# Sparse attention and a soft mixture of experts on one core: local products grouped by key block, dense rows by PE transposes and products over 128 keys

## The chip, the core and the metric

The kernel runs on one NeuronCore of a Trainium2 chip. Its engines are TensorE (PE: matrix products, with weight loads listed apart as PEld), VectorE (DVE), ScalarE (ACT), GpSimd (POOL) and SyncE (SP, which here only starts DMAs). Each engine works through its own queue in order. SBUF is the working memory, PSUM takes the products of PE, and HBM is the main memory. The metric is the device time of one execution in microseconds, lower is better; everything is in float32.

## The reference

For 4 batches, 8 heads, 768 positions and 64 numbers a head, with key blocks of 32 positions (24 blocks):

```python
mask = abs(blk_i - blk_j) <= 1
mask |= (blk_i == 0) | (blk_j == 0) | (blk_i == 23) | (blk_j == 23)
for qb in range(24):
    for kb in sampled_blocks[qb]:        # 3 random key blocks per query block
        mask[qb block, kb block] = True
attn = softmax(where(mask, scale * q @ k.T, -1e9))
x = (attn @ v) as [3072, 512]            # all heads side by side

logits = x @ phi                         # 32 slots: 8 experts of 4
d = softmax(logits over the 3072 rows);  slot_input = d.T @ x
slot_out[e] = relu(slot_input[e] @ w1[e]) @ w2[e]      # w1 512x1024, w2 1024x512
out = softmax(logits over the 32 slots) @ slot_out
```

So query blocks 0 and 23 look at all 768 keys (dense rows), and each of the 22 others at 8 blocks of 32 keys: block 0, block 23, its own with its two neighbours, and three sampled ones. The sampled numbers are read at run time.

## The kernel before

**Local rows.** Two query blocks form a pair, and two pairs a tile of 128 rows of x (T); the first pair of a batch shares its tile with the dense rows. For each query block `stage_k` copies its 8 key blocks side by side into a buffer `kst`: the fixed ones on POOL (L455, L457), the sampled ones on ACT or POOL (L463, L465), for which `block_numbers` loads three numbers from SBUF into the engine's registers (L362). `stage_v` does the same for the sampled value blocks (`vrs`, L481, on POOL). `qk` (L536) makes the scores of a pair: 16 products of 64 rows of the array (a head's 64 numbers) by 32 columns (32 queries), 256 keys each, so that eight of them can lie on the array at once. DVE takes the row maximum (L551), ACT the exponential (L556), and DVE turns the probabilities in blocks of 32 x 32 (L563) into `ptt`. `av_heads` then multiplies them with the values (L628): per tile and half of the heads (r = 0, 1; a *set* below) 44 products with 64 rows, 130 streamed columns (two heads with a column of ones each), and 128, 64 or 32 output columns, depending on how many query blocks share the key block: the two global blocks serve all four query blocks of the tile, the two inner neighbours a pair, all others one query block. Values stand in `vfull` or `vtab` so that two heads fill 64 rows, with zeros for the other head.

**Dense rows.** Per batch there are two dense units, query block 0 and query block 23: scores by products of 64 x 32 with 384 keys (L732), maximum (L750), exponential (L763), DVE transposes into `ptd` (L767), and then, in one piece for both units, `dense`: 24 key blocks x 2 r x 2 g = 96 products of 64 x 64 with 130 columns (`avd`).

**After them** come per tile the division by the sums (L621 to L623, DVE), four transposes by PE (`mxt`, L823) whose result DVE or ACT copies out (`xT`, L374), and per four tiles the logits (`ml`), the exponentials of the dispatch softmax (`lt`, `md`) and the sums over rows (`ms`). The expert products (`pf`, `pso`) and the combination (`po`) follow at the end, fed by 33.5 MB of weights, of which part is loaded early into buffers that the attention has done with (`ktile`, `v0`, `ptd`).

**Order.** All of the attention is written as tasks (`add`). `Plan.run` puts them into one order with a list scheduler that walks through time with a cost per task, a key of due time (`OFF` shifts it by kind), buffer pools and a table of engine delays; the instructions are then recorded in this order, and each engine keeps its part of it. PSUM holds four score banks (`s`), one pair for the products with values (`av`), and two banks (`pt`) for everything that is turned or summed. A float32 product is recorded by the profiler as two products and two weight loads; a transpose is recorded as one of each.

Of the kernel before, what the change touches and what calls it, by code (L numbers as in the profile page):

```python
# [32 lines left out]
EARLYW, LATEW = ("ktile", "v0", "ptd"), ("ktile", "v1")  # L33
# [22 lines left out]
KW = {"ktile": 3, "v0": 6, "v1": 6, "ptd": 3}  # L56
# [6 lines left out]
SWITCH = 0.095  # L63
BACK = {"PE": 0.17, "DVE": -0.07, "ACT": -0.1, "POOL": -0.06, "SP": 0.0, "NONE": 0.0}
OFF = {"acc": 4.15, "av": 2.35, "av1": 4.1, "av2": -5, "avo": -4.9, "avo1": -5, "ce": 5, "cm": -2.05,
       "cn": 0.65, "dav": 3.7, "davo": -3.85, "dexp": 1.8, "do": 2.9, "dqk": 0.05, "dt": 4.55, "dtop": 0.85,
       "dtrn": -4.55, "exp": 2.7, "fix": 4.3, "ldq": 3.55, "lexp": -1.45, "lg": -0.55, "lo": -2.85, "lp": -5,
       "lt": 5, "ltop": -5, "qk": 0.85, "scl": 3.05, "smp": 3.9, "sum": -3.1, "top": -4.8, "trn": 0.2,
       "vst": 4.7, "xt": -2.8, "xto": -1}
# [5 lines left out]
class Task:  # L75
    def __init__(self, f, opts, deps, key, acq, byte, pre, pace, kind, mode, ni):
        self.pace, self.kind, self.mode, self.ni = pace, kind, mode, ni
        self.f, self.opts, self.deps, self.key = f, opts, [d for d in deps if d], key
        self.acq, self.byte, self.pre = list(acq), byte, pre
        self.start = self.fin = self.eng = None  # L80


class Plan:
# [6 lines left out]
    def add(self, f, opts, deps, key, acq=(), byte=0, pre=None, pace=False, kind=None, mode=None, ni=0):  # L90
        t = Task(f, opts if isinstance(opts, list) else [opts], deps, key + OFF.get(kind, 0.0), acq, byte, pre, pace,
                 kind, mode, ni)
        self.tasks.append(t)
        return t

    def run(self):
        tasks = self.tasks
# [3 lines left out]
        left = {t: len(t.deps) for t in tasks}  # L101
        ready = {t: 0.0 for t in tasks}
        out = {t: [] for t in tasks}
        for t in tasks:
            for d in t.deps:
                out[d].append(t)
# [3 lines left out]
        queue = {p: sorted([t for t in tasks if any(q == p for q, _ in t.acq)], key=lambda t: t.key)  # L110
                 for p in self.pools if p not in self.free}
        gives = {t: [] for t in tasks}
        spans, open_ = [], {}
        avail = [t for t in tasks if not t.deps]
        order = []
        while avail:
            cand = []
            for t in avail:
                r, ok, k = ready[t], True, {}
                for p, _ in t.acq:  # L120
                    i = (nxt[p] + k.get(p, 0)) % self.pools[p]
                    k[p] = k.get(p, 0) + 1
                    if (p in queue and queue[p][0] is not t) or held[p][i]:
                        ok = False
                        break
                    r = max(r, slot[p][i])
                if ok:
                    if t.pace:
                        r = max(r, paced)

                    st, e, d = min(((max(r, at[e]), e, d) for e, d in t.opts), key=lambda z: (z[0], z[0] + z[2]))
                    if e == "PE" and t.mode and t.mode[0] != mode:
                        d += SWITCH
                    cand.append((st, t.key, st + d, t, e, d))
            assert cand, [(t.key, t.opts) for t in avail][:8]
            soon = min(c[:3] for c in cand)
# [1335 lines left out]
```

## Time and profile before

| | |
|---|---|
| median of three runs | 306.38 us (304.79 to 307.34) |
| the profiled execution | 307.42 us, its span 305.6 us |
| PE busy in the span | 278.8 us, 7165 products and as many weight loads |
| DVE, ACT, POOL busy | 210.1, 165.1, 184.2 us |
| HBM read and written | 56.19 and 6.29 MB |

Times in the rows below are us from the span's start, unless marked ns. A product is pipelined, and its end is modelled, so PE's busy share says that PE has work, not that the array is full. "Idle before" of a group is the time in which its engine did nothing just before it, with what ended the wait.

### The profile page before, as it was taken

The page shows a single profiled execution, that of the slowest core. Times are in us where ns is not written, and L with a number is a line of the kernel's source. Part 1 is how long each engine was busy: PE and PEld are TensorE (multiplying, and loading weights), DVE is VectorE, ACT ScalarE, POOL GpSimd, SP SyncE. Part 2 cuts the span into 40 slices and gives each one's busy share as a digit, 9 for nine tenths or more (in the row PEclk, how much of TensorE's full clock was granted, in tenths as well). Part 3 has the DMA queues.
Part 4 walks back from the last instruction along what each step waited for, and adds up shares of the span by engine and source line. Part 5 has one row for each costly group of instructions (what it writes and reads, how often), then busy time and mean ns, then how long its engine had stood idle before and what let it go on. Part 6 is the DMA issues. An engine that isn't in the chain of part 4 may idle for free.

```text
span 305.6 us, 17578 instructions
## 1 busy us (share of the span) xinstructions
PE 278.8 (91%) x7165; PEld 193.4 (63%) x7165; DVE 210.1 (69%) x484; ACT 165.1 (54%) x507; POOL 184.2 (60%) x519
## 2 busy tenths in 40 slices
PE   7599998799999999989999899999999999999950
PEld 7158765476687666768676676877657763355540
DVE  4788968458999679878988669999779445012350
ACT  0876848463766875637758653876844142102440
POOL 2679489927954899885689894948957405000000
PEclk9869999999999999999999999999999999999996
DMA  7935677640156663035376510477788999999997
GB/s 244 400 116 161 177 209 222 167 126 3 38 158 193 185 184 105 5 88 139 105 197 190 144 50 28 131 209 208 211 221 288 397 400 408 407 409 407 389 343 263
DMA packets 31634, 63.61 MB, mean 208 GB/s; under 512 B 5313, under 2 KB 18754, under 8 KB 31554
## 3 DMA queue, kind: packets, MB, share of 16 engines
q1 hardware_dynamic: 31408, 62.37, 63.2%
q8 instruction: 56, 0.92, 1.3%
q14 instruction: 24, 0.20, 0.2%
q10 hardware_dynamic: 146, 0.13, 0.1%
HBM read 56.19 MB, written 6.29 MB: 204 GB/s over the span
## 4 chain that ended last, share of the span: by engine, by line
PE 64%; DMA 7%; issue 6%; POOL 6%; DVE 5%; POOLq 5%; ACT 4%; ACTq 1%; SPq 1%
PE av L628 24%; PE avd L628 7%; PE s L536 7%; PE pso L1278 5%; PE pf L1270 5%; PE sd L732 4%; POOLq L362 4%; DMA q<-in_qT_dram 4%; PE mxt L823 3%; PE ml L859 2%; PE ms L910 2%; POOL kst L465 2%; DMA ktile<-in_kT_dram 2%; POOL kst L457 2%; POOL vrs L481 1%
## 5 line engine op out<-in xcount | busy, mean ns | idle before, releaser
L481 POOL COPY vrs<-v 128x260 f32 x264 | 95.1, 407 | 21.2 <-PE av L628 12.2
L556 ACT ACTIVATE p<-s,nm 128x256 f32<-128x256 f32 x176 | 72.8, 483 | 11.3 <-DVE nm L551 9.8
L628 PE MATMUL av<-v,ptt 64*64 64x130 f32 (+2 forms) x1728 | 76.0, 288 | 0.1
L628 PEld LDWEIGHTS av<-v,ptt 64*64 64x64 f32 (+2 forms) x1728 | 50.5, 133 | 24.9 <-issue 16.8
L563 DVE STREAM_TRANSPOSE ptt<-p 128x512 f32<-128x512 f32 x88 | 57.5, 689 | 7.8 <-ACT p L556 7.2
L536 PE MATMUL s<-kst,q 64*32 64x256 f32 x1408 | 51.7, 380 | 7.4 <-POOL kst L465 4.3
L551 DVE TENSOR_REDUCE nm<-s 128x2 f32<-128x512 f32 x88 | 55.1, 680 | 4.6 <-PE s L536 4.2
L457 POOL COPY kst<-ktile 128x384 f32<-128x384 f32 x88 | 43.1, 509 | 11.9 <-PE s L536 11.0
L628 PE MATMUL av<-vrs,ptt 64*32 64x130 f32 x2112 | 46.6, 275 | 2.1 <-issue 1.9
L463 ACT ACTIVATE kst<-ktile 128x128 f32 x165 | 38.3, 310 | 9.1 <-PE s L536 8.7
L536 PEld LDWEIGHTS s<-kst,q 64*32 64x32 f32 x1408 | 29.9, 106 | 20.4 <-POOL kst L465 5.9
L628 PEld LDWEIGHTS av<-vrs,ptt 64*32 64x32 f32 x2112 | 35.6, 105 | 4.5 <-issue 4.3
L374 ACT COPY xT<-mxt 128x512 f32<-128x512 f32 (+1 forms) x25 | 14.1, 566 | 32.7 <-PE mxt L823 32.7
L465 POOL COPY kst<-ktile 128x128 f32 x99 | 24.9, 297 | 0.5 <-ACT kst L463 0.5
L498 ACT ACTIVATE q<-q 128x256 f32<-128x256 f32 x29 | 12.2, 427 | 21.4 <-DMA q<-in_qT_dram 21.4
L628 PE MATMUL avd<-v,ptd 64*64 64x130 f32 x768 | 22.8, 271 | 0.8 <-DVE x L623 0.6
L628 PEld LDWEIGHTS avd<-v,ptd 64*64 64x64 f32 x768 | 21.6, 132 | 2.4 <-PE s L536 2.0
L621 DVE TENSOR_SCALAR rs<-av 128x8 f32<-128x8 f32 (+2 forms) x28 | 4.5, 159 | 23.3 <-PE av L628 23.2
L732 PE MATMUL sd<-ktile,q 64*32 64x384 f32 x256 | 18.6, 524 | 1.1 <-ACT p L556 1.1
L500 POOL TENSOR_SCALAR q<-q 128x256 f32<-128x256 f32 x19 | 7.7, 409 | 18.9 <-DMA q<-in_qT_dram 14.1
L750 DVE TENSOR_REDUCE nm<-sd 128x1 f32<-128x384 f32 x32 | 16.3, 547 | 3.1 <-PE sd L732 3.1
L623 DVE TENSOR_TENSOR x<-av,rs 128x512 f32<-128x512 f32 (+2 forms) x28 | 16.9, 605 | 1.0
(124 smaller groups left out, 288.8 us busy)
## 6 DMA issues: line engine op xcount, KB each, us to landing
w<-in_w_dram SPq DMA_DIRECT2D x20, 512.0 KB, 9.9
v<-in_w_dram SPq DMA_DIRECT2D x12, 512.0 KB, 10.5
q<-in_qT_dram SPq DMA_DIRECT2D x47, 128.0 KB, 2.9
w<-in_w_dram SPq DMA_DIRECT2D x44, 128.0 KB, 3.3
out_dram<-ob SPq DMA_DIRECT2D x22, 256.0 KB, 4.4
ktile<-in_kT_dram SPq DMA_DIRECT2D x48, 96.0 KB, 3.1
v<-in_w_dram SPq DMA_DIRECT2D x24, 128.0 KB, 3.8
kw<-in_w_dram SPq DMA_DIRECT2D x6, 512.0 KB, 8.3
```

The costliest lines, as they stand in the source:

```text
L457: POOL.tensor_copy(out=st[:, :, w:w + 96], in_=kv[:, :, (i - 1) * BLK:(i + 2) * BLK])
L463: ACT.activation(out=st[:, :, o:o + BLK], in_=src, func=AF.Copy, scale=1.0)
L465: POOL.tensor_copy(out=st[:, :, o:o + BLK], in_=src)
L481: POOL.tensor_copy(out=st[:, :, j:j + 1, :], in_=vf[:, :, ds(t.vals[j], 1), :])
L536: PE.matmul(u.s[r][32 * p:32 * p + 32, j, :], lhsT=u.q[s_, p, j, :], rhs=kd[j][0][s_, p, :], start=True, stop=True)
L551: DVE.tensor_reduce(out=u.nm[r], in_=u.s[r], axis=AX.X, op=ALU.max, negate=True)
L556: ACT.activation(out=u.p[r][:, j, :], in_=u.s[r][:, j, :], func=AF.Exp, bias=u.nm[r][:, j:j + 1], scale=1.0)
L563: DVE.transpose(out=T.pt[r][:, :, 2 * w:2 * w + 2, :].rearrange("p k j q -> p j k q"), in_=u.p[r].rearrange("p j (k q) -> p j k q", k=8))
L623: DVE.tensor_tensor(out=x, in0=a[:, :, :, 0:D], in1=rs[lo:hi].unsqueeze(3).to_broadcast([hi - lo, 2, 2 * n, D]), op=ALU.mult)
L628: PE.matmul(av[:, r * 2 * D1:(r + 1) * 2 * D1].rearrange("p (a d) -> p a d", a=2), lhsT=lhsT, rhs=rhs, start=start, stop=stop)
L732: PE.matmul(u.s[r][k][32 * p:32 * p + 32, :], lhsT=T.dq.q[s_, p, j, :], rhs=kt[s_, p, 384 * k:384 * (k + 1)], start=True, stop=True)
L750: DVE.tensor_reduce(out=u.nm[r][:, k:k + 1], in_=u.s[r][k], axis=AX.X, op=ALU.max, negate=True)
```

## The change

- **Local products.** The sampled and fixed key blocks take a place in `kst` that depends on the query block's place t (0 to 3) in its tile: the window of three lies at 64 + 32 t, so a key block that several query blocks of a tile share has one place in all of them. `av_heads` sorts a set's products by width: those for four or three query blocks (128 or 96 columns), for two (64), for one (32); 42 in all. It writes them from wide to narrow, or (`up`) from narrow to wide, whichever begins with the shape that PE is in.
- **Dense rows.** A dense unit is now two heads per half with both dense query blocks (64 queries), not one query block of all heads. Scores are products of 64 x 64. The probabilities are turned by PE, six transposes of 128 x 128 per unit and r into two banks of `pt`, which DVE or ACT copies to SBUF. The products take 128 keys at a time from a new input `vden` (values with a column of ones, by key), 64 output columns and 65 streamed ones, in one task per unit (g = 0, 1).
- **Loads.** `vden` is loaded per batch in 16 pieces (3 whole ones in batch 0) into a buffer `vd`, in place of `ptd` and of nearly its size.
- **Block numbers** are loaded for both query blocks of a pair at once.
- **x** of two tiles is turned in one task of eight transposes.
- **Order.** The list scheduler is replaced by a written table of task numbers (`ORDER`, 1,375 of them), a + behind a number meaning the second choice of engine. A few costs are changed; they affect when registers are loaded and where waits for paced DMAs are put, not the order.

```diff
 class Plan:
...
+        for word in ORDER:
+            t = self.tasks[int(word.rstrip("+"))]
+            e, d = t.opts[word.count("+")]
...
+            if e == "PE":
+                t.up = t.turn and t.mode[0] != mode and t.mode[-1] == mode
...
     def stage_k(b, i, n, use, t_):
...
-            POOL.tensor_copy(out=st[:, :, w:w + 96], in_=kv[:, :, (i - 1) * BLK:(i + 2) * BLK])
+            POOL.tensor_copy(out=st[:, :, 64 + 32 * t_:160 + 32 * t_], in_=kv[:, :, (i - 1) * BLK:(i + 2) * BLK])
...
     def block_numbers(b, t, i, eng, most):
+        j = (i - 1) // 2
+        key = b, most, j, eng
+        if key not in both:
+            _, both[key] = nc.values_load_multi_w_load_instructions(
+                t[0:1, 2 * j + 1:2 * j + 3, :], engines=[{"ACT": E_.Activation, "POOL": E_.Pool}[eng]], min_val=0, max_val=most,
...
     def av_heads(T, rs_, up=False):
...
+        for r in rs_:
+            vb = lambda k: vt[:, :, VPOS(k), r, :]
+            for n, k in enumerate((0, NB - 1)):
+                put(wide, r, 0, n, nt, vb(k))
+            for n in range(nt + 2):
+                k, ts = i0 - 1 + n, range(max(0, n - 2), min(n, nt - 1) + 1)
+                if k in (0, NB - 1):
+                    continue
+                if len(ts) == 3 and ts[0]:
+                    put(low, r, ts[0], 2 + n, 1, vb(k))
+                    ts = ts[1:]
+                put((low, mid, wide)[len(ts) - 1], r, ts[0], 2 + n, len(ts), vb(k))
+        for n in ((1, 2, 0) if up else range(NR)):
             for r in rs_:
+                for t in range(nt):
+                    put(low, r, t, rest(t)[n], 1, us[t // 2].vst[t % 2].st[:, :, n, r, :])
+        todo = low + mid + wide if up else wide + mid + low
...
     def plan_dense(b, j, n):
...
-            def turn(t, r=r):
-                for k in range(2):
-                    DVE.transpose(out=ptd[r][:, 12 * k:12 * k + 12, j, :], in_=u.p[r][k])
...
+            def turn(t, r=r, z=z):
+                z.b = [bank("pdt") for _ in range(2)]
+                for c in range(NT):
+                    PE.transpose(z.b[c // 3][:, c % 3, :], u.p[r][c // 3][:, c % 3 * P:(c % 3 + 1) * P], ident)
+
+            def out(t, r, k, z):
+                if k == 0:
+                    u.pT[r] = pw.tile([P, 8, P], F32, tag="ptt", name="pdt", bufs=PTB)
+                evac(u.pT[r][:, 3 * k:3 * k + 3], z.b[k][:, 0:3], t.eng)
...
+                def dense(t, u=u, g=g, z=z):
+                    z.av = psA.tile([P, 2, 512], F32, tag="av", name="avd", bufs=1)
+                    for c in range(NT):
+                        for a in range(2):
+                            for r in range(2):
+                                PE.matmul(z.av[64 - 64 * r:128 - 64 * r, a, 0:D1], lhsT=u.pT[r][:, c, 64 * a:64 * a + 64],
+                                          rhs=vd[:, c, r * NP + 2 * g + a, :], start=c == 0, stop=c == NT - 1)
```

What stands on PE in the second batch from the first scores after its dense products on: the last `s` of a pair, the turn of a tile (`mxt`), and one set of local products (`av`). Names are output<-inputs, then output columns x streamed columns, then how often in a row. Before:

```order
L536 MATMUL s<-kst_96,q_98 32x256 x8
L823 MATMUL mxt<-ident,x 128x128 x4
L628 MATMUL av<-v_69,ptt 128x130 x4
L628 MATMUL av<-v_69,ptt 64x130 x8
L628 MATMUL av<-v_69,ptt 32x130 x8
L628 MATMUL av<-vrs_103,ptt 32x130 x2
```

And after, where one set of the tile ends and the next begins:

```order
L687 MATMUL av<-v_69,ptt 32x130 x6
L687 MATMUL av<-vrs_105,ptt 32x130 x2
...
L687 MATMUL av<-v_69,ptt 64x130 x6
L687 MATMUL av<-v_69,ptt 96x130 x2
L687 MATMUL av<-v_69,ptt 128x130 x8
L687 MATMUL av<-v_69,ptt 96x130 x2
L687 MATMUL av<-v_69,ptt 64x130 x6
L687 MATMUL av<-v_69,ptt 32x130 x6
```

A set now begins narrow and ends wide, and the next one runs back, so that the two 128-column runs meet without a change of shape; before, each set ran from wide to narrow.

The dense rows of the second batch on PE, before:

```order
L732 MATMUL sd<-ktile,q_98 32x384 x16
...
L536 MATMUL s<-kst_96,q_100 32x256 x8
L628 MATMUL avd<-v_69,ptd 64x130 x96
L536 MATMUL s<-kst_93,q_97 32x256 x8
```

And after:

```order
L804 MATMUL sd<-ktile,q_97 64x384 x8
L850 MATMUL pdt<-ident,pd 128x128 x6
...
L595 MATMUL s<-kst_94,q_99 32x256 x8
L850 MATMUL pdt<-ident,pd 128x128 x6
L873 MATMUL avd<-vd,pdt 64x65 x24
L850 MATMUL pdt<-ident,pd 128x128 x6
L595 MATMUL s<-kst_96,q_100 32x256 x8
```

The one block of 96 dense products has become two of 24, with four sets of six transposes ahead of and between them.

## Rows read from the trace of the kernel before

**Rows 1.** Stages: start:end, length, busy us (and count) by engine, PEclk, DMA share, GB/s.
```profile
18.00:75.00 57.00, 52.54 (x1572) 38.08 (x1568) 43.33 (x91) 36.45 (x111) 43.77 (x126) 0.98 0.52 148
75.00:132.00 57.00, 55.33 (x1715) 40.77 (x1699) 47.08 (x105) 37.34 (x122) 44.30 (x124) 1.00 0.42 116
132.00:189.00 57.00, 54.20 (x1654) 39.86 (x1660) 45.77 (x103) 36.04 (x110) 44.28 (x129) 1.00 0.46 126
189.00:246.00 57.00, 56.31 (x1629) 41.76 (x1614) 45.31 (x108) 31.22 (x99) 39.63 (x110) 1.00 0.77 232
246.00:291.00 45.00, 43.81 (x485) 22.70 (x485) 13.98 (x42) 12.54 (x33) 4.33 (x8) 1.00 1.03 405
```

**Rows 2.** PE in order of time, narrow stretches: start, us, engine, line, op, tiles, shape, count.
```profile
39.91 0.66 PE L823 MATMUL mxt<-ident,x 128*128 128x128 f32 x4
40.50 0.72 PE L628 MATMUL av<-v,ptt 64*128 64x130 f32 x8
82.61 5.62 PE L628 MATMUL avd<-v,ptd 64*64 64x130 f32 x192
88.15 2.06 PE L536 MATMUL s<-kst,q 64*32 64x256 f32 x64
249.85 1.08 PE L1133 MATMUL psS<-selw,sacc 128*128 128x32 f32 x8
```

**Rows 3.** Waits of PE: for whom, us in total, times, the longest.
```profile
PE s L536 <- POOL kst L465: 4.3, 3, 2.8
PE s L536 <- POOL vrs L481: 1.9, 1, 1.9
PE av L628 <- issue: 1.9, 6, 0.7
PE ml L859 <- issue: 1.0, 1, 1.0
PE ml L859 <- ACT xT L374: 0.7, 1, 0.7
```

**Rows 4.** The chain that ended last, 44 to 60 us: shares, and pieces of it.
```profile
by line: POOLq L362 28.6%; issue 18.3%; POOL vrs L481 17.9%; POOL kst L465 9.7%; PE s L536 8.8%; PE av L628 8.2%; POOLq L481 4.0%; POOL kst L457 3.1%; PE mxt L823 1.6%; POOLq L465 0.6%; POOLq L455 0.5%; POOL kst L455 0.5%
...
53.49 0.72 POOLq L362
```

**Rows 5.** From the page: busy us by engine, and the chain of the whole run by line.
```profile
PE 278.8 (91%) x7165; PEld 193.4 (63%) x7165; DVE 210.1 (69%) x484; ACT 165.1 (54%) x507; POOL 184.2 (60%) x519
...
PE av L628 24%; PE avd L628 7%; PE s L536 7%; PE pso L1278 5%; PE pf L1270 5%; PE sd L732 4%; POOLq L362 4%; DMA q<-in_qT_dram 4%; PE mxt L823 3%; PE ml L859 2%; PE ms L910 2%; POOL kst L465 2%; DMA ktile<-in_kT_dram 2%; POOL kst L457 2%; POOL vrs L481 1%
```

**Rows 6.** The same chain at other places: start, us, what.
```profile
15.87 2.35 PE sd L732 x16
...
20.06 1.86 DVE ptd L767 x4
...
135.84 1.04 issue
```

**Rows 7.** DMA queues: kind, packets, MB, share of 16 engines.
```profile
q8 instruction: 56, 0.92, 1.3%
```

**Rows 8.** Weight loads of PE by shape: count, busy us, mean ns, idle before.
```profile
L628 PEld LDWEIGHTS avd<-v,ptd 64*64 64x64 f32 x768 | 21.6, 132 | 2.4 <-PE s L536 2.0 <-DVE ptd L767 0.3
L628 PEld LDWEIGHTS av<-v,ptt 64*128 64x128 f32 x320 | 21.0, 184 | 9.7 <-issue 8.1 <-PE s L536 0.8 <-PE mxt L823 0.3
```

**Rows 9.** DVE and ACT groups by shape, and the page's group of transposes on PE.
```profile
L767 DVE STREAM_TRANSPOSE ptd<-pd 128x384 f32<-128x384 f32 x32 | 16.3, 552 | 1.3 <-ACT pd L763 1.2
L1376 DVE COPY ob<-po 128x512 f32<-128x512 f32 x10 | 6.7, 690 | 7.0 <-PE po L1374 7.0
L556 ACT ACTIVATE p<-s,nm 128x256 f32<-128x256 f32 x176 | 72.8, 483 | 11.3 <-DVE nm L551 9.8 <-issue 0.4 <-DVE ptt L563 0.3
L823 PE MATMUL mxt<-ident,x 128*128 128x128 f32 x96 | 15.9, 286 | 0.1
```

**Rows 10.** PE in the stretch of the lower clock: columns as in rows 1.
```profile
13.57:20.40 6.83, 5.71 (x79) 0.50 0.64 225
```

More of the change, by code (lines that the diff above doesn't have):

```diff
@@ L109, in run @@
         nxt = {p: 0 for p in self.pools}
[L110 to L136, printed above, removed]
-            eng = min(cand, key=lambda c: c[:3])[4]
-            st, _, en, t, e, d = min((c for c in cand if c[4] == eng and c[0] <= soon[0] + 0.05), key=lambda c: c[1:3])
-            avail.remove(t)
-            if e == "PE":
-                mode = t.mode[-1] if t.mode else None
-            t.start, t.eng, at[e] = st, e, en + BACK[e] + (0.11 if t.kind in ("qk", "dqk") else 0.0)
@@ L359, in load_v, with block_numbers @@
         return i
-    def block_numbers(t, i, eng, most):
-        _, vals = nc.values_load_multi_w_load_instructions(
-            t[0:1, i, :], engines=[{"ACT": E_.Activation, "POOL": E_.Pool}[eng]], min_val=0, max_val=most,
-            skip_runtime_bounds_check_because="block numbers lie in range by the definition of the input")
-        return vals
+    both = {}
+    def block_numbers(b, t, i, eng, most):
+        j = (i - 1) // 2
[3 more added lines that the diff above has]
+                t[0:1, 2 * j + 1:2 * j + 3, :], engines=[{"ACT": E_.Activation, "POOL": E_.Pool}[eng]], min_val=0, max_val=most,
+                skip_runtime_bounds_check_because="block numbers lie in range by the definition of the input")
+        o = (i - 2 * j - 1) * NR
+        return both[key][o:o + NR]
     def place(b, t):
@@ L671, in plan_av @@
+        seen = set()
+        for z in todo:
+            r, o, mm, g, lhsT, rhs = z
+            start = rows(z)[0] not in seen
+            assert all((q in seen) != start for q in rows(z))
+            seen.update(rows(z))
+            for q in rows(z):
+                left[q] -= 1
+            av_mm(T.av, o, mm, g, r, lhsT, rhs, start, not any(left[q] for q in rows(z)))
     def plan_av(T, n):
@@ new lines, in plan_dense @@
+            t_t = add(turn, ("PE", 0.6), [t_e], n + 0.3 + 0.01 * r, kind="dtp", mode="F", ni=12,
+                      acq=[("pt", b_use[0]), ("pt", b_use[1]), ("ptt", use)])
+            for k in range(2):
+                p_use[k].append(t_t)
+                t_o.append(add(lambda t, k=k, r=r, z=z, out=out: out(t, r, k, z), [("DVE", 0.5), ("ACT", 0.45)], [t_t] + t_o[-1:], n + 0.35 + 0.01 * r + 0.002 * k, kind="dto"))
+                b_use[k].append(t_o[-1])
+        T.dense.append((u, t_o, pt_use))
```

326 lines of the change are left out of this document (178 added, 148 removed), and 51 rows, old and new, of the table ORDER.

## The prediction

> **What bounds the kernel now.** I read the stages first [rows 1]. Batches 0 to 3 take the four stretches of 57 us between 18 and 246 us, with TensorE (PE) busy for 52.5 to 56.3 us of each, against 43 to 47 for VectorE (DVE) and 40 to 44 for GpSimd (POOL). From 246 us on the expert weights arrive at 405 GB/s while PE works through them; the change touches nothing there, so a gain or a loss must come out of the first 246 us and moves the rest as a block.
>
> PE's busy time is no measure of its work, so I looked at single products [rows 2]. A matrix product in float32 leaves two records. The 192 records of a dense product (`avd`, 64 rows by 64 columns of the array) start at 82.61 and the next task at 88.15: 5.54 us, and as four such tiles fit the array at once that is 48 steps of 0.115. The first eight 64 x 128 records of the local products take 0.72 in all, two at a time, so four steps; less the last one's own 0.27 the three starts between them lie 0.15 apart, the first of which also loads weights. Four transposes (`mxt`) take 0.66 with the last one's 0.29 in it, about 0.12 apart, and the next task begins 0.59 after their start: 0.44 for four steps of 0.11 and 0.15 for the change of shape. I carry 0.11 as the price of a step, whatever the width of the product, and 0.15 for each change of tile shape.
>
> Next, what PE waits for [rows 3]: POOL 4.3 + 1.9 us (2.8 of it one wait at the start), "issue" 1.9 + 1.0, ACT 0.7, and others alike. Idle counts only beyond the modelled end of a product, so each is worth some 0.2 us more. The chain of waits says more about POOL: in 44 to 60 us, 28.6% of the chain is POOLq L362 [rows 4], the loading of block numbers into registers, one of them 0.72 us long, and over the whole run that line alone is 4% of the chain [rows 5], some 12 us. "Issue" on PE (1.04 us at 135.84, between products of one task) [rows 6] waits for no engine: I read it as the supply of instructions. The queue for instructions carried 56 pieces of 0.92 MB together [rows 7], 16 KB a piece, one for every 256 of the 14,330 records of PE and its weight loads [rows 5].
>
> **The change, part by part.** *Local products (L628, av).* Grouped by the place of the key block, a set (one tile, one half of the heads) has 42 products instead of 44: 30 narrow instead of 32, 6 of 64 columns instead of 8, 4 of 128 as before and 2 new ones of 96. In steps that is no saving. Narrow: eight tiles fit at once, and the busiest column still has four products per row half, so 8 steps as before. 64 columns: two of the three key blocks fall on the same column half, so 4 steps as before. Wide: the two 96s take a step each per record, 6 steps instead of 4. Twenty tiles x 2 sets x 2 steps x 0.11 = **+8.9 us**. No row of before has 96 columns; the nearest is the 128-column one, and the price lies between nothing (if the narrow step shrinks as much) and this. I take the upper end, since step time follows what is streamed and the streamed 130 columns stay.
>
> *Dense products.* 48 calls a batch (96 records) of 128 keys x 64 columns x 65 outputs, two at a time, replace 96 calls (192 records) of 64 x 64 x 130, four at a time. The count of steps stays 48 per batch, with half the stream: 0.115 / 2 = 0.058, or 2.8 us instead of 5.54. That shape isn't in the trace. From below it costs the 0.058; from above a step of 0.11, because the eight 128 x 128 products with 32 outputs take 1.08 us less 0.28, still 0.114 apart [rows 2], which is the load of 128 weight columns and not the stream. Here 64 columns are loaded, and 64-column loads last 132 ns against 184 for 128 [rows 8], so I take the lower end: **-11.1 us** in four batches, -0.7 at the other end.
>
> *Transposes by PE.* 96 of them at 0.11: **+10.6 us**. They replace 32 DVE transposes of 0.55 us, 16.3 in all [rows 9]. Their copies out of PSUM (9 on DVE, 23 on ACT) and ten xT copies that move to DVE (0.69 each, as a copy of that size takes; three quarters of it for the others) leave DVE about 5 us better off, and ACT even. The first twelve transposes stand before the second `sd`, where PE now waits until 15.87 us: their 1.3 us is covered, and the DVE chain behind it, which holds the first dense product, loses its 1.86 us of transposes [rows 6]. I count **-2.5 us** for the start; if that cover is gone it is 0.
>
> *Tile shapes.* Counted over both built orders, PE changes shape 210 times before and 215 after. Changes into local products fall from 128 to 105, as one set runs from narrow to wide and the next from wide to narrow, and into `mxt` from 24 to 14, as two tiles are turned together; but the new transposes cost 15, the dense scores and products 10 more, and the scores after a set that ends wide 12 more: **+0.8**. PE's own work is thus 8.9 - 11.1 + 10.6 + 0.8 = **+9.2 us**, more and not less.
>
> Here the Trainium skill speaks against the change. The trace shows 96 transposes 0.11 apart with the granted clock at 1.00 in nearly all of the stretches that hold them [rows 1, 2]. "TensorE: Matmul & The Clock Gate", Part 4: PE-mode transpose, gives about 275 ns for one in a kernel and says that the clock gate does not count transposes as a busy engine; by the 275 the 96 new ones would be an estimated 26 us. The row decides for the price, and the clock is a rival below.
>
> *Instruction supply.* The records fall by 160 (av) + 384 (avd) + 128 (sd, now 64 columns wide) + 14 (fillers) and grow by 96, each with its weight load: -1,180 of 14,330. The listed issue waits are 3.2 us, some 5 with the hidden part; transposes at 0.11 for two instructions are also slow consumers. **-3.5**, between 0 and -5.
>
> *Block numbers.* Loads on POOL fall from 111 to 70 in the built order, on ACT from 55 to 36. Of 12 us of chain that is at most 4.5; with shorter waits elsewhere, and PE being later anyway by its own extra work, I take **-5.5** for all waits on other engines, between -1 and -9.
>
> *Value loads.* `vd` adds 1.6 MB a batch. DMA share is 0.42 to 0.52 in batches 0 to 2 [rows 1], and the last load is for batch 3, before the weights fill the queue, so nothing; uncovered it is 4 us a batch at the 405 GB/s of the end. In batch 0 two q loads now stand behind pieces of `vd` on SP's queue, some 3 us later than now, and their scores come after the first local product, which covers it.
>
> Sum: 9.2 - 3.5 - 5.5 - 2.5 = -2.3. The profiled execution took 307.4 us with a span of 305.6; the median of the three runs is 306.4, so I take 1.0 off: 305.1 profiled, **304.0** as a median, with 300 to 309 as this case's own range.
>
> **The rivals.** *Supply is the bound* (faster). If 18 to 246 us ran at the rate of instructions, 13,110 in 228 us [rows 1] or 17.4 ns each, 1,180 fewer would save 20 us. Half of it, where the array does not hold it up, gives 296. For it: the issue waits, and PE's even density. Against: `avd` ran at 5.54 us for 384 instructions, 14.4 ns each, so supply can do better than the mean.
>
> *The dense chain is exposed* (slower). Six transposes need both PSUM banks of the `pt` pool, and the next six wait until ACT or DVE has copied both out, behind whatever exponentials are queued on ACT (0.48 each [rows 9]). Sixteen sets with 0.6 us exposed are 9.6 us; and PE's fixed order can keep the old waits. It decides from about 5 us of the 15 that this can reach: 311.
>
> *Dense steps do not halve* (slower): the weight load sets them at 0.11, +10.4, 314.
>
> *The clock falls* (slower). Between 13.57 and 20.40 us the granted clock was 0.50 [rows 10], after PE had waited 2.8 us for its first keys [rows 3]. If a stretch of transposes let it fall as long in each batch, that is 4 x 3.4 us, 318. By the skill's Part 4 this is what transposes invite; twelve in a row, 1.3 us, against 24 `mxt` sets that never did it, speak against.
>
> **How the numbers follow.** Forecast 0.45; supply 0.25; exposed chain 0.20; steps not halved 0.07; clock 0.03. A change below 1% (3.1 us) can hardly be told from none here. Faster: 0.25 and the lower 0.19 of the forecast's 0.45. Slower: 0.24 from the last three with the forecast's edge. Same: 0.32. The range 296 to 312 leaves out the clock, the steps and the outer half of two rivals.
>
> **What would show it.** In the profile after, `av` products of 96 columns should stand as 160 records, with a tile's two sets together about 0.4 us longer in steps; `avd` as 384 records in sets of 48 that take 1.4 to 1.5 us (2.7 would be the weight load); `pdt` sets of six about 0.7. PE's waits for POOL at L513 and L522, and POOLq on the chain, should halve; "issue" before av should nearly vanish; waits of `avd` or `pdt` for a `pdt` copy are the exposed chain. The stretch 75 to 246 us, three batches, tells all this best. I am wrong if the 96-column products cost no step, or if the new order leaves PE waiting for copies.

## The result, and the profile after

The changed kernel takes 308.62 us (median of 20 runs, 306.27 to 311.68) against 306.89 for the kernel before (20 runs, 304.79 to 310.99): a ratio of 1.0084, 95% interval 1.0055 to 1.0113. By this ratio it is slower by some 2.6 us where 2.3 us of gain was forecast. The ratio leaves out executions that the record marks as slow, so it differs a little from the ratio of the medians. The profiled execution took 309.22 us with a span of 307.4, and the experts at the end begin 1.6 us later (`psS` at 251.44 us for 249.85); behind that both kernels take as long.

The stages after, columns as in [rows 1]:

```profile
18.00:75.00 57.00, 55.74 (x1492) 39.63 (x1490) 45.15 (x96) 37.13 (x121) 44.90 (x127) 0.97 0.64 190
75.00:132.00 57.00, 53.20 (x1499) 39.91 (x1496) 45.43 (x99) 37.98 (x115) 46.27 (x135) 1.00 0.52 147
132.00:189.00 57.00, 55.73 (x1531) 40.71 (x1530) 45.62 (x104) 37.63 (x117) 43.90 (x128) 1.00 0.54 156
189.00:246.00 57.00, 53.25 (x1466) 40.79 (x1464) 43.61 (x106) 29.59 (x90) 39.57 (x114) 1.00 0.80 238
```

PE's busy time is what it was, with 7 to 13% fewer records of products in each of the last three stretches. By the page ([rows 5] has it before), busy us by engine:

```profile
PE 278.6 (91%) x6575; PEld 196.0 (64%) x6575; DVE 206.1 (67%) x479; ACT 165.7 (54%) x504; POOL 187.6 (61%) x535
```

So PE works 0.2 us less and stands idle 2.0 us more (28.8 us of the span for 26.8). The loss comes late: the dense scores of the last batch begin at 178.3 us, 1.6 earlier than before, and from there to `psS` it takes 73.1 us against 70.0. From 178 to 252 us PE waits 2.8 us for `kst` after the change, and no wait is listed there before. PE in order of time around the dense products of the second batch (columns as in [rows 2], in brackets the wait ahead), then the last sets of local products on the chain (start, us, what):

```profile
79.92 0.87 PE L850 MATMUL pdt<-ident,pd 128*128 128x128 f32 x6
80.73 1.62 PE L873 MATMUL avd<-vd,pdt 128*64 128x65 f32 x48
82.28 0.87 PE L850 MATMUL pdt<-ident,pd 128*128 128x128 f32 x6
...
89.48 0.88 PE L595 MATMUL s<-kst,q 64*32 64x256 f32 x24 [1.27 <-POOL kst L522]
```

```profile
232.37 2.60 PE av L687 x81
...
237.10 2.58 PE av L687 x78
```

Six transposes take 0.81 us from their start to the next task's, and 48 records of `avd` 1.55, each with one change of shape. A set of local products takes 2.58 us here; what it took before is read further down, where the grouping stands alone. The second dense scores of the first batch begin late, at 19.12 us where they began at 15.87 [rows 6]:

```profile
19.12 2.67 PE L804 MATMUL sd<-ktile,q 64*64 64x384 f32 x16
```

PE's waits, as [rows 3]:

```profile
PE s L595 <- POOL kst L522: 9.7, 6, 3.8
PE pdt L850 <- ACT pd L835: 1.1, 1, 1.1
PE av L687 <- issue: 0.7, 1, 0.7
PE ml L963 <- issue: 0.6, 1, 0.6
```

"Issue" before `av` and `ml` fell from 2.9 to 1.3 us, the way of the forecast, and the waits on POOL rose from the 6.2 us of [rows 3] to 9.7 where they were to halve. The chain from 85 to 110 us (first fence) runs on POOL almost alone; a third of it is "issue", POOL idle with no cause in the profile. On the whole chain (second fence, before and after) POOL and POOLq have 17%, 11% before:

```profile
by line: issue 33.4%; POOL vrs L540 18.7%; POOLq L404 17.2%; POOL kst L522 14.4%; POOL kst L513 9.5%; POOLq L522 2.4%; POOLq L540 2.0%; POOL kst L511 1.4%; POOL q L559 1.1%; ACT kst L520 0.8%; POOLq L511 0.4%; POOLq L513 0.3%
```

```profile
PE 64%; DMA 7%; issue 6%; POOL 6%; DVE 5%; POOLq 5%; ACT 4%; ACTq 1%; SPq 1%
PE 58%; POOL 12%; issue 10%; POOLq 5%; DVE 4%; ACT 4%; DMA 3%; ACTq 1%; DVEq 0%
```

The line that answers it: the register loads of block numbers by themselves (engine, operation, what is read, count: shortest/median/longest in ns, first and last start). First before, then after:

```profile
L362 POOLq TENSOR_LOAD <-vreg x88: 722/728/753, 13.7 to 232.5; - x88
L362 POOLq TENSOR_LOAD <-sreg x33: 723/732/932, 8.7 to 213.6; - x33
```

```profile
L404 POOLq TENSOR_LOAD <-vreg x44: 1382/1388/1400, 15.7 to 227.7; - x44
L404 POOLq TENSOR_LOAD <-sreg x30: 1382/1388/1597, 8.9 to 215.9; - x30
```

A load of six numbers lasts 1.39 us, one of three 0.73. POOL loads 74 x 6 = 444 numbers in place of 121 x 3 = 363 (a pair's key numbers are loaded twice where one half is copied by ACT and the other by POOL), and its loads take 103 us instead of 88. ACT's loads grow as well: 36 of 1.33 us, 48 in all, for 55 of 0.70, 39 in all.

### The profile page after: what moved, and what is told of

It reads as the page before. It is cut to its first block, busy times and chain, and to the rows that moved or that the text cites. A ratio compares the mean times of both kernels' runs of the same rounds, so it can differ in the third digit from the quotient of the medians.

```text
span 307.4 us, 16300 instructions
## 1 busy us (share of the span) xinstructions
PE 278.6 (91%) x6575; PEld 196.0 (64%) x6575; DVE 206.1 (67%) x479; ACT 165.7 (54%) x504; POOL 187.6 (61%) x535
## 4 chain that ended last, share of the span: by engine, by line
PE 58%; POOL 12%; issue 10%; POOLq 5%; DVE 4%; ACT 4%; DMA 3%; ACTq 1%; DVEq 0%
PE av L687 21%; PE s L595 7%; PE pso L1383 5%; PE pf L1375 5%; POOL vrs L540 4%; POOLq L404 4%; PE sd L804 3%; POOL kst L513 3%; POOL kst L522 3%; PE pdt L850 3%; PE st L439 2%; PE ml L963 2%; PE po L1479 2%; PE mxt L915 2%; DMA q<-in_qT_dram 2%
## 5 line engine op out<-in xcount | busy, mean ns | idle before, releaser
L540 POOL COPY vrs<-v 128x260 f32 x264 | 94.2, 404 | 25.1 <-PE av L687 14.7
L687 PE MATMUL av<-v,ptt 64*64 64x130 f32 (+3 forms) x1568 | 82.8, 282 | 1.3 <-DVE x L682 0.7
L615 ACT ACTIVATE p<-s,nm 128x256 f32<-128x256 f32 x176 | 71.2, 480 | 22.1 <-DVE nm L610 14.7
L687 PEld LDWEIGHTS av<-v,ptt 64*64 64x64 f32 (+3 forms) x1568 | 59.6, 137 | 22.0 <-issue 14.9
L595 PEld LDWEIGHTS s<-kst,q 64*32 64x32 f32 x1408 | 27.4, 107 | 26.0 <-POOL kst L522 12.9
L520 ACT ACTIVATE kst<-ktile 128x128 f32 x150 | 34.1, 303 | 10.8 <-PE s L595 9.7
L522 POOL COPY kst<-ktile 128x128 f32 x114 | 28.4, 294 | 1.8 <-issue 1.7
L835 ACT ACTIVATE pd<-sd,nb 128x384 f32<-128x384 f32 x32 | 16.8, 588 | 8.3 <-DVE nb L830 6.7
L417 ACT COPY pdt<-pdt 128x384 f32<-128x384 f32 x23 | 10.5, 480 | 13.9 <-PE pdt L850 13.1
L850 PE MATMUL pdt<-ident,pd 128*128 128x128 f32 x96 | 15.5, 301 | 1.1 <-ACT pd L835 1.1
L850 PEld LDWEIGHTS pdt<-ident,pd 128*128 128x128 f32 x96 | 11.2, 150 | 6.8 <-issue 3.0
L557 ACT ACTIVATE q<-q 128x256 f32<-128x256 f32 x28 | 11.1, 418 | 7.7 <-DMA q<-in_qT_dram 6.7
L804 PE MATMUL sd<-ktile,q 64*64 64x384 f32 x128 | 13.8, 544 | 0.0
```

Source lines behind the costliest of these rows:

```text
L520: ACT.activation(out=st[:, :, o:o + BLK], in_=src, func=AF.Copy, scale=1.0)
L522: POOL.tensor_copy(out=st[:, :, o:o + BLK], in_=src)
L540: POOL.tensor_copy(out=st[:, :, j:j + 1, :], in_=vf[:, :, ds(t.vals[j], 1), :])
L595: PE.matmul(u.s[r][32 * p:32 * p + 32, j, :], lhsT=u.q[s_, p, j, :], rhs=kd[j][0].st[s_, p, :], start=True, stop=True)
L615: ACT.activation(out=u.p[r][:, j, :], in_=u.s[r][:, j, :], func=AF.Exp, bias=u.nm[r][:, j:j + 1], scale=1.0)
L687: PE.matmul(av[:, r * 2 * D1:(r + 1) * 2 * D1].rearrange("p (a d) -> p a d", a=2), lhsT=lhsT, rhs=rhs, start=start, stop=stop)
```

## The experiments

Ratios are to the kernel before, timed on the same chip beside each kernel, with 95% intervals. These chips spread wider than the one of the result (the kernel before: medians of 308 to 310 us), so intervals are 0.4 to 0.8% to either side. The kernel after was not timed again on them: another kernel is compared with it through the ratios (after: 1.0084), which takes it that a ratio holds from chip to chip. First theory: PE's steps and the waits on POOL, each as read above.

### The steps: 96-column products split, local part alone

```diff
+                if len(ts) == 3:
+                    put(low, r, ts[2], 2 + n, 1, vb(k))
+                    ts = ts[:2]
```

> The kernel after, with each key block that three query blocks share split into a product of 64 columns and one of 32, so that no product of 96 columns is left: 44 products a set, 16 steps instead of 18. If a 96-column record takes a whole step of the array and PE's steps set the time (theory), a tile's two sets fall from 4.93 us to about 4.5 and the run loses up to 40 sets x 2 steps x 0.11 = 8.9 us, to 300 to 303 us, faster than both kernels. If PE is paced by POOL's copies (first rival), sets get shorter, but the waits for kst take it up: 306 to 309 us. If the supply of instructions is the bound (second rival), 160 records more, with as many weight loads, cost 160 x 2 x 17.4 ns = 5.6 us: 312 to 315 us.

Measured 1.0071 (0.9989 to 1.0152): no gain. The chain at the end shows why:

```profile
228.37 2.37 PE av L687 x87
...
231.77 2.40 PE av L687 x86
...
239.47 2.27 PE av L687 x69
241.74 2.85 issue
```

Sets are back at 2.4 us, from 2.6 at the same place of the kernel after, so the step price of the 96 columns is right: two steps, 0.2 us. But the last one stops for 2.85 us on "issue", and PE's waits for issue before `av` are 5.9 us in all, for 0.7 us with 96 columns. This execution took 311.34 us, longer than most of its kernel; the two other splits below show the same rise, 2.1 to 5.3 and 1.5 to 4.7 us. What the array gives back, the supply of instructions takes.

That these stops are supply can be read from their places. Counted over PE's instructions as the trace lists them, 86 of the 87 stops on "issue" above 0.3 us, in all 20 traces, fall on the 194th or 195th of a group of 256, whatever PE works on there. The queue for instructions brought 52 pieces after the change, one for every 256 of 13,324.

The local grouping alone, in the kernel before (places in `kst`, `av_heads` of after; its list scheduler and all else kept, and every set still written from wide to narrow):

> The kernel before with the local products alone grouped by the place of the key block (96-column products, 42 a set); list scheduler, dense rows and block numbers as before. If a 96-column record takes a whole step (theory), 40 sets get 0.22 us longer: +7 to +9 us on PE, 312 to 316 us. If products cost by their columns or by their number (rival), nothing changes or it is a little faster: 304 to 308 us.

Measured 1.0009 (0.9967 to 1.0051). The theory as stated fails: the steps got longer and the time did not. The same tile (both sets) in the two chains, first before, up to the next task at 234.48 us, then grouped, up to 234.57:

```profile
229.32 4.67 PE av L628 x169
233.99 0.07 issue
234.06 0.43 PE av L628 x7
```

```profile
229.38 5.18 PE av L631 x161
```

That is 5.16 and 5.19 us. Over the whole traces, from a set's first record to the next task, the 20 sets that stand alone took 2.31 us before (median; the shortest 2.17) and 2.51 grouped (2.39): the two steps. Of the ten tiles whose two sets follow on each other the shortest took 4.62 and 5.06 us, four steps, but the median is 5.19 in both: before, the same work took anything up to 5.53. PE's busy time rose by 5.4 us, from 278.8 to 284.2, and its idle time fell by 3.7: "issue" before `av` from 1.9 to 1.0 us, and "issue" before `ml` is gone from the list. That the 160 records saved are what pays for the steps fits this; no run separates it from the other waits that shrank.

### The start

```diff
+            if b == j == 0 and 1 in ks:
+                st = bank("st")
+                for _ in range(18):
+                    PE.matmul(st[:, 0, :], lhsT=ident, rhs=ident, start=True, stop=True)
```

> The kernel after, with 18 filler products of 128 x 128 on PE behind the first dense scores of batch 0, so that PE is not idle from 8.5 to 12.76 us of the span. Their result is read by nobody. If the idle time is what brings the granted clock down to 0.50 for 10.2 us (theory), the clock stays at its upper level there, or comes back earlier, and the run loses 2 to 4 us: 304.5 to 306.5 us. If the clock falls whatever PE does there, or if the start is set by the loads alone (rival), the time stays at 308 to 309 us.

Measured 1.0095 (1.0045 to 1.0146): no gain. The stretches of [rows 10], after and with the fillers (column 8 is the granted clock):

```profile
6.70:13.60 6.90, 3.13 (x34) 1.26 (x41) 2.26 (x6) 4.51 (x15) 3.98 (x11) 0.83 1.04 403
13.60:20.40 6.80, 5.71 (x51) 3.23 (x39) 3.62 (x6) 4.15 (x12) 3.80 (x11) 0.50 1.03 393
20.40:27.30 6.90, 6.59 (x180) 4.17 (x174) 5.60 (x16) 4.28 (x13) 5.60 (x17) 0.92 0.26 83
```

```profile
6.70:13.60 6.90, 6.90 (x80) 5.44 (x86) 2.26 (x6) 4.59 (x15) 4.00 (x11) 1.00 1.03 404
13.60:20.40 6.80, 5.04 (x55) 2.39 (x37) 4.27 (x7) 4.08 (x11) 4.35 (x13) 0.78 1.03 393
```

Here the clock follows PE's idle time: kept busy, PE has 0.78 for 0.50 in the second stretch. The time does not follow the clock of this stretch.

### The loads and copies of POOL

Before, with the merged loads alone (`block_numbers` of after):

> The kernel before with the block numbers loaded for both query blocks of a pair at once, and nothing else. By the forecast's term (waits for POOL shrink with the loads of numbers) it gains 3 to 5 us: 302 to 304 us. If POOL's copies and not its register loads set PE's waits, or if PE's own work fills the time (theory now), it stays within 1 us of before: 306 to 308 us.

Measured 1.0043 (0.9998 to 1.0088). There is no gain; its trace has 69 loads of 1.39 us on POOL, 96 us where before has 88.

Next, both kernels without the sampled copies and without loads (PE reads what the first use of each buffer left there):

> The kernel after without the sampled copies (keys and values are copied into each buffer at its first use only, from fixed places, and no block numbers are loaded), so that PE reads old blocks and POOL has little left to do. If POOL's staging is what PE waits for in the middle (theory: the waits that rose from 12.7 to 16.9 us up to the experts), most of them go and the run loses 8 to 12 us: 297 to 301 us. If the array's steps and the supply of instructions fill the time anyway (rival), it loses at most 3 us: 306 or more.

> The kernel before, with the sampled copies and the block numbers left out in the same way. This and the lean version of after show what is left when POOL is out of the way: PE's own work and the supply of instructions. By the forecast's prices (+9.2 of steps, -3.5 of supply) the lean after should be 5 to 6 us slower than the lean before; if the two lean kernels differ by less than 1.5 us, the change costs PE nothing by itself; if the lean before is the slower one, fewer instructions are worth more than the steps.

> The lean kernel after, with the products of 96 columns split into 64 and 32. With POOL out of the way the price of the 96-column record shows in the time: by steps (theory) 8.9 us less than the lean after; by the supply of instructions (rival) 160 records more at 2 x 17.4 ns, up to 5.6 us more; both at once, something between -4 and 0.

Measured 0.9872 (0.9803 to 0.9941) for after, 0.9932 (0.9884 to 0.9980) for before, 0.9962 (0.9914 to 1.0009) for after without 96 columns. POOL's busy time fell from 187.6 to 74.5 us, and after gained 2.1%, before 0.7%. With POOL out of the way the change is no loss (0.994 of the lean before, less than the intervals can tell). Splitting the 96 columns again gained nothing (0.9% longer, the intervals just overlap), with issue waits before `av` at 5.3 us for 2.1. Of the two expectations neither came: after got some 6 us shorter, less than the 8 to 12 of the theory and more than the 3 of its rival.

So copies or loads? Fixed numbers (2, 9, 17 for every query block) in place of loaded ones, all copies kept:

> The kernel after with fixed block numbers (2, 9, 17 for all query blocks) in place of those read from SBUF into registers: all copies stay, the register loads on POOL and ACT go. If the loads of numbers are what makes POOL late (theory A), most of the 2.1% that the lean version gained over after comes already here: 302 to 304 us on a chip where before takes 307. If it is the copies and their place in the written order (theory B), it gains less than 1.5 us.

> The kernel before with fixed block numbers in the same way. The forecast priced all of these loads at up to 12 us of the chain and 4.5 us of that for the change: by it this kernel gains 4 us or more. If the loads stand beside PE's own work, it gains 0 to 2 us, like the lean version of before (0.7%).

Measured 0.9850 (0.9793 to 0.9906) for after and 1.0060 (1.0018 to 1.0103) for before. In after the loads, with the register operations that go with them (378 on POOL, 17 us), are all of what the lean kernel gained; the copies, 111 us of POOL's busy time, are worth nothing beside that (theory A). In the kernel before the same loads cost nothing. There it is leaving out the copies as well that gains, 0.993 for 1.006; that fixed numbers alone came out slightly slower is not explained. Fixed numbers take away ACT's loads too, 48 us of them in after, and no run separates the two engines' loads; in after's chain from 18 to 75 us ACT's (ACTq L404) are 5.2%.

More loads, one group at a time:

> The kernel after with the block numbers loaded for one query block at a time again, as before: 111 loads on POOL instead of 70. By the forecast's term it is 4 to 5 us slower than after. If the loads are not what PE waits for, it stays within 1.5 us of after; if the loads for two query blocks at once come late for the first of them, it is 1 to 2 us faster.

Measured 1.1110 (1.1057 to 1.1163). The edit changed the key under which a pair's numbers are kept, from the pair to the query block, and so each of the 126 loads on POOL still took six numbers, 1.39 us each: 175 us of loads, twice what was meant. It is no undoing of the merge, but the strongest dose of loads: +72 us of them on POOL made the kernel 31 us longer.

```profile
PE s L595 <- POOL kst L522: 14.4, 8, 5.1
```

The merge undone as it should be (three numbers, one query block), and the same overdose in the kernel before:

> The kernel after with the loads of block numbers exactly as before: three numbers for one query block, where after loads the six of a pair (the earlier run with one load per query block had by its trace still loaded six at a time, 1.39 us each, 126 times on POOL). The traces give 0.73 us for a load of three on POOL and 1.39 for one of six, so POOL spends 126 x 0.73 = 92 us on loads in place of 74 x 1.39 = 103. If a number costs the same however it is loaded (theory), merging saved nothing, and this is 0 to 4 us faster than after. If the number of loads counts (the forecast's step), it is 3 to 5 us slower than after.

> The kernel before with six numbers loaded for every query block, of which three are used: POOL spends 121 x 1.39 = 168 us on loads in place of 88, the dose that made the written order 31 us slower. If before's order has slack on POOL for loads (theory: fixed numbers gained it nothing), it loses at most 8 us; if POOL is as close to the bound in both orders (rival), 25 us or more.

Measured 1.0029 (0.9956 to 1.0101) and 1.0921 (1.0847 to 1.0994). Undoing the merge is no loss, as the theory has it, and rather a gain of 0.5%, which the intervals do not separate from after. The theory of slack in the kernel before is wrong beyond its present dose: +80 us of loads cost it 28 us, as the rival said.

Fewer numbers to load: DVE packs the three of a query block into one, and the engine takes them apart.

```diff
+        _, (p,) = nc.values_load_multi_w_load_instructions(t[0:1, i:i + 1], ...)
+        return [... for v in (p & 31, (p >> 5) & 31, p >> 10)]
```

> The kernel after with the three numbers of a query block packed by DVE into one number at the start, so that one register is loaded per query block and taken apart by three register operations. At (1.39 - 0.73) / 3 = 0.22 us a number a load should take 0.29 us, 126 of them 37 us, and 378 register operations at about 0.05 us 19 us: 56 us in place of 103. If the loads on POOL are what after's order waits for (theory), about half or more of the 2.3% between after and the version with fixed numbers comes back: 303 to 306 us where before takes 307 to 309. If register operations cost as much as the numbers did (rival), nothing: 309 to 311.

> The kernel before with packed block numbers (one register loaded per query block, 121 loads of 0.29 us and 363 register operations on POOL in place of 121 loads of 0.73). If the order of before hides the 88 us of loads that it has (theory: fixed numbers gained nothing there, doubling cost 28 us), it stays within 0.7% of before, and the packed kernel after is the faster of the two by what the change is worth without its loads. If loads cost something in before's order as well (rival), it gains 1% like the packed kernel after, 304 to 306 us where before takes 308 to 309.

Measured 0.9983 (0.9933 to 1.0033) for after, apart from its 1.0084 by more than both intervals, and 1.0024 (0.9985 to 1.0064) for before. The loads and register operations of the packed kernel after:

```profile
L404 POOLq TENSOR_LOAD <-vreg x88: 281/288/302, 14.6 to 223.9; - x88
```

```profile
L541 POOLq ALU_OP  x264: 32/35/35, 15.3 to 230.8; - x132
```

What POOL then waits for, after and packed (executions of 309.22 and 304.38 us): it has got its slack back.

```profile
POOL vrs L540 <- PE av L687: 14.7, 8, 4.6
POOL q L559 <- DMA q<-in_qT_dram: 8.1, 6, 3.8
POOL kst L513 <- PE s L595: 7.7, 11, 1.6
```

```profile
POOL vrs L541 <- PE av L688: 20.4, 11, 5.4
POOL q L560 <- DMA q<-in_qT_dram: 18.7, 8, 3.4
POOL kst L514 <- PE s L596: 10.2, 12, 2.0
```

The traces also show what the dose alone hides. From 18 to 232 us most of POOL's register work (loads and register operations) lies under its own copies, and only what lies outside them adds to its time: 9 of 101 us before, 15 of 107 with the merged loads there, 21 of 115 after, 6 of 105 with the merge undone, 1 of 69 packed. A load of 1.39 us is too long for the copy before it more often than one of 0.73 (a reading; POOL's spans are rough). Loads on POOL (count x median) against the ratio, in one table:

| us of loads on POOL | kernel before | kernel after |
|---|---|---|
| 0 (fixed numbers) | 1.006 | 0.985 |
| 35 to 36 (packed) | 1.002 | 0.998 |
| 88 / 92 (three numbers) | 1 | 1.003 |
| 96 / 103 (six, pairs) | 1.004 | 1.008 |
| 168 / 175 (six, each) | 1.092 | 1.111 |

### Dense rows alone, and the supply of instructions

The kernel before with the new dense rows (scores, transposes, `avd`, `vd`) in its list scheduler's order:

> The kernel before with the new dense rows alone (scores 64 columns wide, transposes by PE, products over 128 keys, vd in place of ptd), in the order of its list scheduler; local products and block numbers as before. By the forecast's prices PE's work changes by -11.1 + 10.6 + about 1 for shapes and the supply by about -3: 304 to 308 us, no change. If the copies out of PSUM stand between the transposes and the products (the exposed chain), or the written order is what pays, 2 to 5 us slower: 309 to 312.

Measured 1.0665 (1.0581 to 1.0749), 20 us slower. Its PE waits:

```profile
PE mxt L851 <- DVE x L630: 4.4, 4, 3.5
PE s L543 <- ACT q L505: 3.5, 1, 3.5
PE pdt L786 <- ACT pd L771: 3.1, 1, 3.1
PE pdt L786 <- DVE pdt L376: 2.4, 3, 0.9
```

`pdt` waits for exponentials and for copies out of the banks, 6.0 us with the smaller ones, and tiles behind them for theirs: the exposed chain. The same tasks in after wait 1.1 us at this place. But PE's busy time rose too, from 278.8 to 290.4 us, and the granted clock was below 1.00 in stretches where before and after have 1.00 (columns as in [rows 1]):

```profile
132.00:189.00 57.00, 52.21 (x1428) 36.97 (x1428) 41.90 (x97) 33.60 (x102) 39.44 (x113) 0.94 0.46 132
246.00:270.00 24.00, 21.59 (x434) 16.21 (x433) 10.63 (x38) 4.24 (x14) 10.73 (x28) 0.93 1.00 349
```

In the first of them it stood at 0.50 for 6.8 us from 137.0 us on, beside the wait of 3.5 us for `x`. How the 20 us divide among these was not tried.

More instructions with next to no streaming:

```diff
+            if mm == BLK and left[rows(z)[0]]:
+                pads[0] += 1
+                if pads[0] % 6 == 0:
+                    PE.matmul((T.av[g][o:o + mm] if isinstance(T.av, list) else T.av[o:o + mm, g])[:, r * 2 * D1:r * 2 * D1 + 1],
+                              lhsT=lhsT, rhs=vt[64 * g:64 * g + 64, 0, VPOS(NB), r, 0:1], start=False, stop=False)
```

> The kernel after with 177 extra products among the narrow local ones, each 64 rows by 32 columns with a single streamed column of zeros added to a sum that is open, so that it changes nothing: 354 records and as many weight loads, 708 instructions, with next to no streaming. If the supply of instructions is what the local products run at (theory), they cost 14 to 17 ns each: 10 to 12 us more than after. If the array's steps set the pace, an eighth of a step each: 177 x 2 x 0.11 / 8 = 5 us at most, 0 to 2 if a narrow step with one column is short.

Measured 1.0284 (1.0212 to 1.0356), 2% or some 6 us over after: 35 ns a product (20 to 50 by the intervals), between both prices and settling neither. PE's issue waits before `av` are 3.4 us for 0.7.

### Once POOL has slack

> The kernel after with packed block numbers and the 18 filler products at the start. In the kernel after the fillers brought the start forward by about 1 us, and it was gone by 84 us. If POOL took it up (theory), it stays now that POOL has time to spare: 1 to 3 us faster than the packed kernel alone, ratio to before 0.988 to 0.995. If something else takes up the start, such as the q loads (rival), the ratio is that of the packed kernel, 0.998.

> The packed kernel after, with the products of 96 columns split into 64 and 32. In the kernel after and in its lean version the split took 5 us off the local products and put as much into waits for instructions (2.6 to 7.8 and 5.4 to 9.5 us). If the supply of instructions takes the steps up (theory), the ratio stays within 0.5% of the packed kernel's 0.998. If POOL had hidden the gain in the first of these runs (rival), 4 to 5 us faster: 0.982 to 0.986.

Measured 1.0036 (0.9991 to 1.0081) and 0.9991 (0.9913 to 1.0069). With the fillers the granted clock did not fall at the start, and still nothing came of it:

```profile
13.60:20.40 6.80, 5.03 (x114) 3.55 (x113) 5.90 (x11) 4.60 (x13) 4.72 (x15) 1.00 1.04 399
20.40:27.30 6.90, 4.65 (x131) 3.31 (x121) 3.94 (x12) 5.09 (x15) 5.50 (x16) 1.00 0.35 103
```

PE is busy for only 4.65 us of the later stretch, at full clock: at 22.88 us it stands for 2.25 us on "issue" inside the first local products. And the clock fell later, as the page's row of it shows (tenths, 40 slices of the span):

```profile
PEclk9999999899999799999999999999999999999976
```

The two dips are stretches at 0.50, 3.4 us each, from 53.1 and from 100.9 us on; PE had just waited 2.7 us for `vrs` and 2.0 for q. So the fillers move a fall of the clock, and no run shows what the start alone is worth. The split again moves the gain to issue (`av` waits 4.7 us for 1.5). No kernel that computes everything is faster than before beyond the interval; the packed one is faster than after and level with before. The three packed kernels are 0.6 to 1.0% below their unpacked twins, one of the three beyond the intervals.

## Why the prediction was wrong

**The step that failed is "Block numbers", the -5.5 for all waits on other engines.** It read a cost per load out of [rows 4, 5] and counted loads, 111 to 70 (121 and 74 in the traces). A load costs by its numbers, 0.29, 0.73 and 1.39 us for one, three and six, and the change loads more of them: 88 to 103 us of POOL. PE's listed waits on POOL rose by 3.5 us instead of falling, and the merge alone, in the kernel before, gained nothing (1.004). Fixed numbers take 2.3% off after and nothing off before, packed ones 1.0% and nothing. The second mistake in the same step is the reading of the chain: 12 us of POOLq on it said that POOL was late behind something, not that the time would shrink with the loads; in before they could all go without gain. With the loads as before (three numbers) the change is level with before (1.003), with fixed numbers in both it is 2.1% faster, so this term holds the gain back; that the merge alone turned the sign is within the intervals and not shown.

Why before gains nothing from fewer loads and after does is only partly shown. POOL in before waits 14.1, 12.2 and 11.0 us for q loads, `av` and `s`, in after 8.1, 14.7 and 7.7; and in the last stretch, where after loses its time, the 2.8 us of waits for `kst` are 0.6 with three numbers or packed ones. Which tasks of the written order lost the slack, how much of it is ACT's, and why fixed numbers gain 1.3% more than packed ones in after, was not tried.

**The number was closer than the working.** The forecast had PE's own work up by 9.2 us and the rest down by 11.5. PE's busy time, a rough measure of its work, fell by 0.2 us, and its idle time rose by 2.0. Two misses of some 9 and 13 us largely cancelled; that the forecast lay within 5 us of the result is luck.

**Local products, +8.9.** The price of a step held: 0.2 us a set for two, wherever a set runs undisturbed. But steps and supply were added as if both were paid. Splitting the 96 columns in three kernels gained nothing, and the grouping alone cost 0.1%. By the forecast's terms it would have been 8.9 less about 1 of supply: some 8 us, 2.6%, where the interval ends at 0.5%. The changes of shape, 23 fewer into local products, are not in that kernel. In after, where they are, `av` keeps PE busy for 1.9 us more from 18 to 246 us (112.5 for 110.7).

**Supply, -3.5.** The issue waits fell by 1.6 us listed; beyond the trace, its worth is bound to the steps above.

**Dense products, -11.1.** Right: the two sets of a batch take 1.40 us each and 0.15 for the shape, 3.1 us for the 5.54 of [rows 2]; the steps did halve, as its lower end had it. In four batches that is -9.8 with the shapes.

**Transposes, +10.6.** Right: 0.81 us for six is 6 x 0.11 and 0.15. The rival of an exposed chain did not happen in after (1.1 us), and did in part when the dense rows stood in the list scheduler's order, 20 us slower with lower clocks. That kernel and after differ in the order and in the local products; that the written order is what avoids the waits, for which the forecast had no price of its own, is likely and not shown.

**Start, -2.5.** The cover was gone: PE idled to 12.76 us, waiting 3.8 for `kst`, the clock stood at 0.50 for 10.2 us instead of 6.8, and the second dense scores began 3.3 us later. The forecast's own exception, 0, was still too kind at this place; the kernel had made it up by 64.5 us, where the dense scores of the second batch begin 2.2 us earlier than before.

**Rivals.** "Supply is the bound" is half right: it does not set the whole stretch, but it takes back whatever the local products gain in steps. Steps that do not halve and a clock that falls in each batch did not happen in after (its clock is 1.00 from 75 us on); in eight other traces the clock fell in mid-run, in the two looked at beside waits of PE of 2.0 to 3.5 us.

## What to carry to other kernels

Before pricing a merge of small instructions, look whether the cost goes by the instruction or by the element: one row with the median duration at the old size, and one test at the new. An engine's share of the chain of waits is not what can be gained there; replacing the work by constants on both kernels shows what it is worth in each, and here the same loads were free in one and 2.3% in the other. Two limits that lie close together (array steps and instruction supply) are not two terms of a sum: take the larger, and expect that a cut in one shows up as waits for the other. And take the price of a task from all its occurrences: tiles of the same work took 4.62 to 5.53 us in one trace.

## What the runs showed of the hardware

- A register load on GpSimd lasts 0.29, 0.73 and 1.39 us for one, three and six numbers, about 0.07 + 0.22 a number; on ScalarE 0.28, 0.70 and 1.33. A register operation lasts 35 to 46 ns, so packing pays. Most of this runs under GpSimd's copies: 92 of 101 us before, 68 of 69 packed.
- A product of 64 x 96 takes a whole step, like one of 64 x 128: two of them lengthen a set by 0.2 us (2.37 to 2.40 us without, 2.58 to 2.60 with).
- "Issue" stalls of TensorE come at one place in every 256 of its instructions (86 of 87 above 0.3 us). They reached 2.85 us at 241.74 us of the span, in the stretch in which weights arrive, where the other before a product in that chain was 0.5 us.
- 177 products of one streamed column each cost 35 ns a piece in the time (20 to 50 by the intervals), though their records last 164 ns.
- The granted clock fell to 0.50 for 3.4 us beside waits of PE of 2.0 and 2.7 us (packed, with fillers), and for 6.8 us beside one of 3.5 (dense rows alone).
